# Attention as a software pipeline with an order fixed by hand on four engines, with scores as one float32 product and the sinks' values loaded later

## The chip, the cores and the metric

The kernel runs on one core of one Trainium2 chip. The metric is the device time of one execution in microseconds (us), 719.29 before the change. A core has TensorE (PE, the matrix engine), VectorE (DVE), ScalarE (ACT), GpSimd (POOL) and SyncE (SP, which here only issues DMA transfers). Each engine works through its own instructions in order; semaphores hold an instruction back until what it needs is there.

## The reference

Attention of 2 batches, 8 heads, 768 positions, 64 numbers a head; a query sees the last `window` keys (128) and the first `n_sink` (4). Then two MLPs over the 1,536 tokens. The weights come as float64.

```python
def _attn_ref(q, k, v, n_sink, window):
    scores = scale * np.matmul(q, k.transpose(0, 1, 3, 2))
    keep = (pos < n_sink) | ((rel >= 0) & (rel < window))
    scores = np.where(keep, scores, -1000000000.0)
    a = np.exp(scores - np.max(scores, axis=-1, keepdims=True))
    a = a / (np.sum(a, axis=-1, keepdims=True) + 1e-09)
    return np.matmul(a, v).astype(np.float32)
def _moe_ref(x, w_in, w_out):            # 512 -> 2048 -> 512
    h = x @ w_in
    return (h * (1.0 / (1.0 + np.exp(-1.702 * h))) @ w_out)
def _moe2_ref(x, w_gate, w_val, w_out):  # 512 -> 1536 -> 512
    return (1.0 / (1.0 + np.exp(-(x @ w_gate))) * (x @ w_val) @ w_out)
```

## The kernel before

**Attention** goes in 24 units: a batch b, a block t of 256 queries (3 to a batch) and a pair p of heads (4). A block of t > 0 has 272 columns of keys for each half of 128 queries (its window and 16 columns for the sinks); a first block (t = 0) has 128 and 256. A unit goes through four stages, each a generator:

- `st_a` (L241): four transposes bring q and k of the pair onto 64 partitions a head (tile tqk, L250). ScalarE casts them to the high part (L255), VectorE subtracts for the low part (L257); both stand in kq[p]. GpSimd copies the former block's last 128 keys (L246).
- `st_b` (L262): for each half e and head j the scores s are three products of parts, high with high, high with low, low with high (L278), the two heads in turn. VectorE adds the mask and takes the maximum (L283), ScalarE exponentiates and sums (L291), VectorE makes the reciprocal (L294, L295), GpSimd multiplies (L298) and copies the sinks' columns (L301).
- `st_c` (L305): four transposes of probabilities a head (three in a first block; tile tp, L315), copied to pt by ScalarE (L319), and one of the sinks' (ts, L324, psk, L327).
- `st_d` (L330): the values. o is a float32 product of v and pt for both heads, which fill different halves of o's partitions (L347); the last eight products of a unit are the sinks' with the tile vsk, on 32 rows each. ScalarE casts x to xh (L355), VectorE subtracts to xl (L357).

`load_vsink` (L167) sets vsk of a batch to zero and loads it. Every pass of the loop puts the four stages of four units in turn by the string `order`, with lags 0, 1, 3, 4; but the program is made with `TileContext(nc, schedule_with_timeline_sim=True)` (L725), and that scheduler puts each engine's instructions into an order of its own.

**Weights** come as blocks of four tiles of 128 x 512 (`weight_block`, L77): SP loads a raw tile of float64; ScalarE makes its absolute value (L100), VectorE builds float32 in three operations (L103 to L105), ScalarE casts to the high part (L107), GpSimd subtracts for the low part (L108). A product of the MLPs is `mm3` (L127), three matmuls of parts. The first block of w_in is converted in the attention loop (`W` in `order`).

**The MLPs.** `mlp_h(g)` (L359) multiplies the first block of w_in with 256 finished tokens: 48 matmuls of 256 columns (tile ha) and two copies to yacc (L372). Behind it come the other blocks of the first MLP: h (512 columns a matmul), silu, a split into two parts (L428, L429), and the second products y; then the second MLP in the same way. A block's second products are emitted behind the next block's first tile.

Of the kernel before, what the change touches and what calls it, by code (L numbers as in the profile page):

```python
# [8 lines left out]
F32 = mybir.dt.float32  # L9
# [29 lines left out]
def fast_path(ctx, tc, ident, nwv, any_, q, k, v, n_sink, window, w_in, w_out, w_gate, w_val, w_out2, out):  # L39
# [30 lines left out]
    # what the fast path rests on, checked at the end: the sizes of the weights'  # L70
    # exponents, and each row's maximum
# [5 lines left out]
    def weight_block(src, nm, pool):  # L77
        """A block's tiles, and the steps that fill them: float64 words to float32
        (exponent moved, mantissa cut to 24 bits), then hi + lo."""
        wh = pool.tile([P, 4, 512], F32R, tag="wh", name=f"wh_{nm}")  # L80
        wl = pool.tile([P, 4, 512], F32R, tag="wl", name=f"wl_{nm}")

        def load(i):
            raw = stg.tile([P, 512, 2], I32, tag="raw", bufs=2, name=f"raw_{nm}_{i}")
            nc.sync.dma_start(raw, src[:, i, :].bitcast(I32).rearrange("p (f t) -> p f t", t=2))
            return raw

        def steps():
            raws = [load(0)]
            yield  # L90
            for i in range(4):
                if i < 3:
                    raws.append(load(i + 1))
                raw = raws[i]
                lo, hi = raw[:, :, 0], raw[:, :, 1]
                w = stg.tile([P, 512], I32, tag="w", bufs=2, name=f"w_{nm}_{i}")
                wf = w.bitcast(F32)
                n = len(nbig)
                nbig.append(nm)
                nc.scalar.activation(wf, hi.bitcast(F32), AF.Abs, scale=2.0 ** -112,  # L100
                                     accum_out=big[:, n : n + 1])
# [39 lines left out]
    ps_t = es.enter_context(tc.tile_pool(name="ps_t", bufs=3, space=PSUM))  # L141
    ps_s = es.enter_context(tc.tile_pool(name="ps_s", bufs=3, space=PSUM))
# [4 lines left out]
    qk, vs, vsk = {}, {}, {}  # L147
# [18 lines left out]

    def load_vsink(b):  # L167
        """v of the sinks, for the rows (head of the pair, half of the block, sink)."""
        vsk[b] = ap_.tile([4 * NS, NPAIR, 2, D], F32, tag="vsk", bufs=1, name=f"vsk_{b}")
        nc.gpsimd.memset(vsk[b], 0.0)  # L170
        for j in range(2):
            for e in range(2):
                r = (2 * j + e) * NS
                nc.sync.dma_start(vsk[b][r : r + NS, :, e, :],
                                  v[b, j::2, :NS, :].rearrange("h s d -> s h d"))

# [62 lines left out]
    prs, pts, sks = {}, {}, {}  # L239

    def st_a(b, t, p):  # L241
        """q.T and k.T of a pair of heads, each in two parts."""
        qs, ks = qk[b, t]
        kk = kq[p]
        if t:
            nc.gpsimd.tensor_copy(kk[:, :, :P], f32(kk[:, :, C0 + P : C0 + QB]))  # L246
        tp = ps_t.tile([P, 2, QB], F32, tag="t", name=f"tqk_{b}_{t}_{p}")
# [5 lines left out]
        yield  # L253
        own = kk[:, :, C0:].rearrange("p s (u c) -> p s u c", u=2)
        nc.scalar.copy(own[:, 0], tp)  # L255
        yield
        nc.vector.tensor_tensor(own[:, 1], tp, f32(own[:, 0]), ALU.subtract)  # L257
        if t == 0:
            nc.gpsimd.tensor_copy(kk[:, :, P : P + NS], f32(kk[:, :, C0 : C0 + NS]))
        yield  # L260

    def st_b(b, t, p):  # L262
        """scores, and their softmax over the kept keys."""
        pr = prs[b, t, p] = ap_.tile([P, 2, 2, QB + NS], F32, tag="pr", bufs=2, name=f"pr_{b}_{t}_{p}")
        st = ap_.tile([P, 2, 2, 2], F32, tag="st", bufs=2, name=f"st_{b}_{t}_{p}")
        nm = nmax[:, (b * NQB + t) * NPAIR + p, :]
        if t:
            sks[b, t, p] = ap_.tile([P, 2, 2, NS], F32, tag="sk", bufs=3, name=f"sk_{b}_{t}_{p}")
        for e in range(2):
            mask = (me, mo)[e] if t else (m0, m1)[e]  # L270
            c0 = (e * P if t else C0)      # the first of the columns of keys
            n = QB + NS if t else (P if e == 0 else QB)
            ss = [ps_s.tile([P, QB + NS], F32, tag="s", name=f"s_{b}_{t}_{p}_{e}_{j}") for j in range(2)]
            qsl = slice(Q0 + e * P, Q0 + (e + 1) * P)
            for i, (qi, ki) in enumerate(((0, 0), (0, 1), (1, 0))):
                for j in range(2):
                    hd = slice(64 * j, 64 * j + 64)
                    nc.tensor.matmul(ss[j][:, :n], kq[p][hd, qi, qsl], kq[p][hd, ki, c0 : c0 + n],  # L278
                                     start=i == 0, stop=i == 2)
            yield  # L280
            for j in range(2):
                it = 2 * e + j
                nc.vector.tensor_tensor_reduce(  # L283
                    out=pr[:, j, e, :n], in0=ss[j][:, :n], in1=mask[:, :n], scale=-scale, scalar=3.4e38,
                    op0=ALU.add, op1=ALU.min, accum_out=nm[:, it : it + 1],
                )
            yield
            for j in range(2):
                it = 2 * e + j
                pt = pr[:, j, e, :n]  # L290
                nc.scalar.activation(pt, pt, AF.Exp, bias=nm[:, it : it + 1], scale=-1.0,  # L291
                                     accum_out=st[:, e, 0, j : j + 1])
                yield
            nc.vector.tensor_scalar(st[:, e, 1, :], st[:, e, 0, :], 1e-9, None, ALU.add)  # L294
            nc.vector.reciprocal(st[:, e, 1, :], st[:, e, 1, :])  # L295
            for j in range(2):
                pt = pr[:, j, e, :n]
                nc.gpsimd.tensor_scalar(pt, pt, st[:, e, 1, j : j + 1], 1.0, ALU.mult, ALU.mult)  # L298
            if t:
                at = P if e == 0 else 0  # L300
# [429 lines left out]
```

## Time and profile before

| | before |
|---|---|
| median of 3 runs | 719.29 us (719.19 to 719.37) |
| span of the profiled execution | 719.9 us |
| PE busy, matmuls | 704.8 us (98%), 3574 |
| VectorE busy | 392.9 us (55%) |
| ScalarE busy | 304.0 us (42%) |
| GpSimd busy | 161.3 us (22%) |

The profile is one execution; its own time is the span, from the first instruction to the last. The busy time of PE counts a matmul from its start to a modelled end, so that matmuls that follow each other overlap; starts are better marks than ends. The granted clock is a share of TensorE's full 2.4 GHz. A row of the view by lines tells the line, the engine, the operation, the tiles written and read, the shapes and the count, then busy time and mean ns; in a timeline a row has its start and its time in us.

### The profile page before, as it was taken

How to read it: one execution, taken by the hardware profiler on the slowest of the kernel's cores; microseconds unless marked ns; L12 is line 12 of the kernel's file. 1: busy time of each engine (PE TensorE's matmuls, PEld its weight loads, DVE VectorE, ACT ScalarE, POOL GpSimd, SP SyncE). 2: the span in 40 equal slices, each digit the busy share in tenths (PEclk: the TensorE clock that was granted, in tenths of full speed). 3: DMA queues.
4: the chain of work that ended last, by engine and by line, in shares of the span. 5: the costliest groups of instructions: out<-in, count | busy, mean ns of one | idle time of the engine just before them, and what ended most of it. 6: DMA issues, size and time to landing. Idle time of an engine off the chain costs nothing.

```text
span 719.9 us, 9655 instructions
## 1 busy us (share of the span) xinstructions
PE 704.8 (98%) x3574; PEld 562.1 (78%) x3574; DVE 392.9 (55%) x817; ACT 304.0 (42%) x714; POOL 161.3 (22%) x235
## 2 busy tenths in 40 slices
PE   7999999999999999999999999999998999999995
PEld 4667777778877788888888888888886888888884
DVE  5778766453999847835885781113774225222222
ACT  4787867666664424424443552223441203111110
POOL 4556653332232203101300220001330002000000
PEclk7899999999999999999999999999999999999998
DMA  9754572000333403400420140000441000001101
GB/s 213 157 132 108 149 168 81 2 1 1 102 119 106 141 1 100 135 1 1 145 89 0 60 144 32 1 0 1 147 146 60 0 1 1 0 20 40 39 21 63
DMA packets 49928, 49.08 MB, mean 68 GB/s; under 512 B 39504, under 2 KB 39760, under 8 KB 49872
## 3 DMA queue, kind: packets, MB, share of 16 engines
q1 hardware_dynamic: 49264, 48.24, 23.8%
q8 instruction: 30, 0.49, 0.3%
q14 instruction: 26, 0.21, 0.1%
q10 hardware_dynamic: 544, 0.13, 0.1%
q0 software_dynamic: 64, 0.00, 0.1%
HBM read 45.22 MB, written 3.15 MB: 67 GB/s over the span
## 4 chain that ended last, share of the span: by engine, by line
PE 80%; DVE 7%; DMA 7%; ACT 4%; issue 1%; POOL 1%; ACTq 0%; SPq 0%; POOLq 0%; DVEq 0%
PE s L278 6%; PE o L347 6%; PE g L129 4%; PE y L129 4%; PE y L130 4%; PE o L131 4%; PE o L129 4%; PE g L130 4%; PE o L130 4%; PE y L131 4%; PE g L131 4%; PE v L130 4%; PE v L129 4%; PE v L131 4%; PE tp L315 4%; PE h L129 3%
## 5 line engine op out<-in xcount | busy, mean ns | idle before, releaser
L480 DVE TENSOR_TENSOR sv<-v,sv 128x512 f32<-128x512 f32 x36 | 24.8, 689 | 113.8 <-PE v L131 113.8
L130 PE MATMUL y<-gl,wh_o 128*128 128x512 f32 x192 | 75.2, 393 | 0.3 <-DVE gl L429 0.3
L131 PE MATMUL y<-gh,wl_o 128*128 128x512 f32 x192 | 75.0, 391 | 0.0
L129 PE MATMUL y<-gh,wh_o 128*128 128x512 f32 x192 | 73.0, 394 | 0.9 <-DVE yacc L460 0.5
L479 ACT ACTIVATE sv<-g 128x512 f32<-128x512 f32 x36 | 21.4, 594 | 90.4 <-PE g L131 90.4
L298 POOL TENSOR_SCALAR pr<-pr,st 128x272 f32<-128x272 f32 (+2 forms) x96 | 47.8, 511 | 51.2 <-DVE st L295 23.1
L129 PE MATMUL o<-wh_p,gh_v 128*128 128x512 f32 (+1 forms) x148 | 57.1, 386 | 1.9 <-ACT gh_v L428 1.9
L130 PE MATMUL o<-wl_p,gh_v 128*128 128x512 f32 (+1 forms) x148 | 57.1, 386 | 0.0
L131 PE MATMUL o<-wh_p,gl_v 128*128 128x512 f32 (+1 forms) x148 | 57.1, 387 | 0.0
L129 PE MATMUL g<-xh,wh_g 128*128 128x512 f32 x144 | 57.0, 396 | 0.0
L130 PE MATMUL g<-xl,wh_g 128*128 128x512 f32 x144 | 56.8, 394 | 0.0
L131 PE MATMUL g<-xh,wl_g 128*128 128x512 f32 x144 | 56.7, 394 | 0.0
L131 PE MATMUL v<-xh,wl_v 128*128 128x512 f32 x144 | 56.5, 392 | 0.0
L130 PE MATMUL v<-xl,wh_v 128*128 128x512 f32 x144 | 56.5, 392 | 0.0
L129 PE MATMUL h<-xh,wh_i 128*128 128x512 f32 x144 | 56.5, 392 | 0.0
L129 PE MATMUL v<-xh,wh_v 128*128 128x512 f32 x144 | 56.5, 392 | 0.0
L131 PE MATMUL h<-xh,wl_i 128*128 128x512 f32 x144 | 56.4, 392 | 0.0
L130 PE MATMUL h<-xl,wh_i 128*128 128x512 f32 x144 | 56.4, 392 | 0.0
L428 ACT CAST gh_v<-sv 128x512 fp32r<-128x512 f32 x36 | 22.3, 620 | 78.8 <-DVE sv L480 75.7
L278 PE MATMUL s<-kq 64*128 64x272 f32 (+2 forms) x288 | 52.3, 335 | 1.8 <-DVE kq L257 1.1
L291 ACT ACTIVATE pr<-pr,nmax 128x272 f32<-128x272 f32 (+2 forms) x96 | 47.6, 498 | 14.6 <-DVE nmax L283 13.7
L108 POOL TENSOR_TENSOR wl_p<-w_p,wh_p 128x512 fp32r<-128x512 f32 x12 | 15.9, 1334 | 152.7 <-ACT wh_p L107 152.7
(138 smaller groups left out, 1531.6 us busy)
## 6 DMA issues: line engine op xcount, KB each, us to landing
raw_i<-in_moe_w_in_dram SPq DMA_DIRECT2D x16, 512.0 KB, 4.1
raw_o<-in_moe_w_out_dram SPq DMA_DIRECT2D x16, 512.0 KB, 3.2
raw_g<-in_moe_w_gate_dram SPq DMA_DIRECT2D x12, 512.0 KB, 3.6
raw_v<-in_moe_w_val_dram SPq DMA_DIRECT2D x12, 512.0 KB, 3.6
raw_p<-in_moe_w_out_dram SPq DMA_DIRECT2D x12, 512.0 KB, 3.3
v<-in_v_dram SPq DMA_DIRECT2D x12, 256.0 KB, 5.1
out_dram<-oacc SPq DMA_DIRECT2D x11, 256.0 KB, 2.0
k<-in_k_dram SPq DMA_DIRECT2D x10, 256.0 KB, 4.6
```

Source lines behind the costliest of these rows:

```text
L108: nc.gpsimd.tensor_tensor(wl[:, i, :], wf, f32(wh[:, i, :]), ALU.subtract)
L129: nc.tensor.matmul(ps, ah, bh, start=first, stop=False)
L130: nc.tensor.matmul(ps, ah, bl, start=False, stop=False)
L131: nc.tensor.matmul(ps, al, bh, start=False, stop=last)
L278: nc.tensor.matmul(ss[j][:, :n], kq[p][hd, qi, qsl], kq[p][hd, ki, c0 : c0 + n], start=i == 0, stop=i == 2)
L291: nc.scalar.activation(pt, pt, AF.Exp, bias=nm[:, it : it + 1], scale=-1.0, accum_out=st[:, e, 0, j : j + 1])
L298: nc.gpsimd.tensor_scalar(pt, pt, st[:, e, 1, j : j + 1], 1.0, ALU.mult, ALU.mult)
L315: nc.tensor.transpose(tp[:, o, :], pr[:, j, e, c0 : c0 + P], ident)
L347: nc.tensor.matmul(o[64 * j : 64 * j + 64, cs], vf(2 * p + j), pf(j), start=i == 0, stop=i == len(steps) - 1,)
L428: nc.scalar.copy(h, src)
L479: nc.scalar.activation(sg, pss[0], AF.Sigmoid)
L480: nc.vector.tensor_tensor(sg, pss[1], sg, ALU.mult)
```

## The change

A table of letters (ORDER) replaces the generators and their order string. A letter is one action on one engine with a lag in units: c, T, t copy the former keys, transpose q and k, copy tqk out; S, m, x the scores, maxima and exponentials of half 0 or 1; i, n the reciprocal and the multiplication; P, p transposes and copies of the probabilities of head 0 or 1; K, k the sinks'; V, h, l the values, xh and xl. An H1 (four in a step) gives a group of three ha matmuls, W a piece of a weight conversion. Inside `tc.manual_schedule` the instructions of PE, ACT, DVE and POOL keep the order in which they are written; SP's DMA issues, and all behind the loop, are the scheduler's as before.

```diff
+ORDER = "c-0 i-2 n-2 S0-1 S1-1 m0-1 m1-1 W1 x0-1 V-4 h-4 x1-1 T-0 t-0 H1 l-4 P0-3 H1 W1 p0-3 P1-3 p1-3 H1 H1 K-3 k-3 W1"
+LOADS = (2, 3)
+W_FROM = 4
...
-    ps_t = es.enter_context(tc.tile_pool(name="ps_t", bufs=3, space=PSUM))
-    ps_s = es.enter_context(tc.tile_pool(name="ps_s", bufs=3, space=PSUM))
+    ps_t = es.enter_context(tc.tile_pool(name="ps_t", bufs=2, space=PSUM))
+    ps_s = es.enter_context(tc.tile_pool(name="ps_s", bufs=4, space=PSUM))
...
-        vsk[b] = ap_.tile([4 * NS, NPAIR, 2, D], F32, tag="vsk", bufs=1, name=f"vsk_{b}")
-        nc.gpsimd.memset(vsk[b], 0.0)
+    vsk = kt_p.tile([P, NPAIR, 2, 2, D], F32, name="vsk")
+    sinks = [kt_p.tile([P, P], F32, name=f"sk{i}") for i in range(3)]
...
-    kq = [kt_p.tile([P, 2, Q0 + QB], F32R, name=f"kq{p}") for p in range(NPAIR)]
+    kq = [kt_p.tile([P, Q0 + QB], F32, name=f"kq{p}") for p in range(NPAIR)]
...
-        nc.scalar.copy(own[:, 0], tp)
-        nc.vector.tensor_tensor(own[:, 1], tp, f32(own[:, 0]), ALU.subtract)
+        nc.vector.tensor_copy(kk[:, C0:], tqs.pop(u).rearrange("p u c -> p (u c)"))
...
-            for i, (qi, ki) in enumerate(((0, 0), (0, 1), (1, 0))):
-                for j in range(2):
-                    nc.tensor.matmul(ss[j][:, :n], kq[p][hd, qi, qsl], kq[p][hd, ki, c0 : c0 + n],
-                                     start=i == 0, stop=i == 2)
+        for j in range(2):
+            nc.tensor.matmul(ss[j][:, :n], kq[p][hd, qsl], kq[p][hd, c0 : c0 + n], start=True, stop=True)
...
-            nc.vector.tensor_scalar(st[:, e, 1, :], st[:, e, 0, :], 1e-9, None, ALU.add)
-            nc.vector.reciprocal(st[:, e, 1, :], st[:, e, 1, :])
+        nc.vector.tensor_scalar(st[:, 1], st[:, 0], 1e-9, None, ALU.add)
+        nc.vector.reciprocal(st[:, 1], st[:, 1])
...
-            nc.scalar.copy(pt[:, o0:, :], tp[:, o0:, :])
+        (nc.vector.tensor_copy if j else nc.scalar.copy)(pt[:, o0:, :], tp[:, o0:, :])
...
-                              lambda h, e=e: vn[2 * NS * (h % 2) : 2 * NS * (h % 2 + 1), h // 2, e, :],
-                              lambda j: pt[2][2 * NS * j : 2 * NS * (j + 1), :]))
+                steps.append((slice(e * P, (e + 1) * P), lambda j, e=e: vsk[:, p, j, e, :], lambda j: ps))
...
+    with tc.manual_schedule(engines=engines):
+        for i in range(len(units) + last):
...
+            if u and u[1:] == (1, 0):
+                load_vsink(u[0])
+            for o in order:
+                if o[0] == "H":
+                    h_some(int(o[1:]), max(0, i - last) // NPAIR if w_done[0] >= W_ALL else 0)
+                elif o[0] == "W":
+                    if i >= W_FROM:
+                        w_some(int(o[1:]) * (2 if w_done[0] < W_ALL else 1))
```

Further: vsk and the sinks' tiles are set to zero once, with zero rows so that a sinks' product takes all 128 rows; vsk of a batch is loaded in step 4 and step 16, when the former batch's last unit (unit 11, in step 15) has read it, where before it was set and loaded with the batch's first block. pr has 3 buffers (2), pt 4 (3). Conversions of three blocks of weights (the first of w_in and of w_out, the second of w_in) run in the loop: two pieces for each W until the first block is through, then one, so that a tile takes two steps; VectorE's three operations on a tile are pieces of their own. The ha products stand in the loop from step 8 on, those of the last block behind it.

PE in the steady loop before, at the scores of batch 0's last block: tp are transposes of probabilities, s_2_1 and s_2_2 the scores of pairs 1 and 2 of the last block, kq keys and queries, ha the first MLP's products, tqk transposes of k and q.

```order
L278 MATMUL s_2_1_1_1_850<-kq_157 128x272 x3
L315 MATMUL tp_2_0_0_872<-ident,pr_2_0_724 128x128 x4
L278 MATMUL s_2_2_0_0_889<-kq_158 128x272
L278 MATMUL s_2_2_0_1_890<-kq_158 128x272
L131 MATMUL ha_1_2000<-xh_80,wl_i_161 128x256
L129 MATMUL ha_1_2000<-xh_80,wh_i_160 128x256
L130 MATMUL ha_1_2000<-xl_83,wh_i_160 128x256
L250 MATMUL tqk_2_3_880<-ident,k_2_491 128x128 x2
```

The same place after the change: a whole step's first half, where unit (2, pair 1) is scored.

```order
L291 MATMUL s_2_1_0_0_739<-kq_165 128x272
L291 MATMUL s_2_1_0_1_740<-kq_165 128x272
L291 MATMUL s_2_1_1_0_743<-kq_165 128x272
L291 MATMUL s_2_1_1_1_744<-kq_165 128x272
L384 MATMUL o_1_2_757<-pt_1_2_0_703,v_0_1_254 64x256
L384 MATMUL o_1_2_757<-pt_1_2_1_710,v_0_1_254 64x256
L384 MATMUL o_1_2_757<-pt_1_2_0_703,v_0_1_255 64x128
L384 MATMUL o_1_2_757<-pt_1_2_1_710,v_0_1_255 64x128
```

The first row of before shows three products of one head alone (x3): of 64 such triples of 272 columns, 51 stand as one row. After, four single products of two heads in turn stand together, and the values follow.

VectorE after the change in step 21: L305 are the maxima, L110, L112, L114 the three operations of a weight tile, L279 and L353 the copies out of tqk and tp.

```order
L305 ISA pr_2_1_1695,nmax<-s_2_1_1_0_1691,mo 128x272
L305 ISA nmax 128x1
L110 TENSOR_SCALAR w_o_0_2364<-w_o_0_2364 128x512
L305 ISA pr_2_1_1695,nmax<-s_2_1_1_1_1692,mo 128x272
L305 ISA nmax 128x1
L112 SCALAR_TENSOR_TENSOR w_o_0_2364<-raw_o_0_2360,w_o_0_2364 128x512
L114 SCALAR_TENSOR_TENSOR w_o_0_2364<-raw_o_0_2360,w_o_0_2364 128x512
L279 COPY kq_166<-tqk_2_2_1719 128x512
L398 TENSOR_TENSOR xl_85<-o_1_2_1705,xh_82 128x256
L110 TENSOR_SCALAR w_i_3_1701<-w_i_3_1701 128x512
L353 COPY pt_1_3_1_1746<-tp_1_3_1_1741 128x512
```

A tile of w_o that is written behind the loop (w_o_0_2364) has been put between a step's own operations; another stands so in step 23.

PE after the change behind the last unit's values: h is the first MLP's second block of features, ha_0_2037 and ha_1_2063 the last block of tokens, y the first second products.

```order
L384 MATMUL o_2_3_2005<-psk_2_3_2003,vsk 64x128 x4
L138 MATMUL ha_1_1973<-xh_82,wh_i_168 128x256
...
L138 MATMUL h_0_0_2396<-xh_80,wh_i_172 128x512
...
L140 MATMUL ha_0_2037<-xh_82,wl_i_169 128x256
L138 MATMUL h_0_2_2436<-xh_80,wh_i_172 128x512
...
L140 MATMUL ha_1_2063<-xh_82,wl_i_169 128x256
L138 MATMUL y_0_0_2134<-gh_0_0_2109,wh_o_170 128x512
```

Behind the values stand 12 matmuls of ha, then 48 of h and 48 of ha in turns of 27, 24, 21 and 24, and then y.

## Rows read from the trace of the kernel before

**Rows 1.** Busy time by stretches (us, count of each engine; then granted clock, DMA).

```profile
60.00:80.00 20.00, 20.00 (x174) 15.72 (x174) 15.05 (x47) 15.99 (x47) 13.21 (x23) 1.00 0.73 184
...
400.00:420.00 20.00, 20.00 (x88) 16.34 (x88) 16.42 (x25) 11.74 (x25) 7.29 (x6) 1.00 0.33 102
```

**Rows 2.** PE's waits over the whole span: us in total, times, longest.

```profile
PE o L129 <- ACT gh_v L428: 1.9, 1, 1.9
PE tqk L250 <- DMA k<-in_k_dram: 1.4, 2, 0.7
```

**Rows 3.** PE by line and form, 0 to 200 us: MLP matmuls of 512 columns.

```profile
L129 PE MATMUL y<-gh,wh_o 128*128 128x512 f32 x18 | 7.0, 389 | 0.0
...
L129 PE MATMUL h<-xh,wh_i 128*128 128x512 f32 x16 | 6.2, 390 | 0.0
```

**Rows 4.** PE's timeline, 60 to 63 us.

```profile
60.21 0.60 PE L315 MATMUL tp<-ident,pr 128*128 128x128 f32 x4
60.74 1.09 PE L347 MATMUL o<-pt,v 128*64 128x256 f32 x12
61.76 0.65 PE L347 MATMUL o<-psk,vsk 32*64 32x128 f32 x8
62.35 0.39 PE L129 MATMUL ha<-xh,wh_i 128*128 128x256 f32 x1
62.57 0.28 PE L130 MATMUL ha<-xl,wh_i 128*128 128x256 f32 x1
62.69 0.28 PE L131 MATMUL ha<-xh,wl_i 128*128 128x256 f32 x1
```

**Rows 5.** PE's timeline at scores, near 65 and 74 us.

```profile
64.67 0.64 PE L278 MATMUL s<-kq 64*128 64x272 f32 x3
65.24 0.66 PE L315 MATMUL tp<-ident,pr 128*128 128x128 f32 x4
...
73.61 0.65 PE L278 MATMUL s<-kq 64*128 64x272 f32 x6
74.18 0.43 PE L347 MATMUL o<-psk,vsk 32*64 32x128 f32 x2
```

**Rows 6.** VectorE's timeline, 61 to 63 us.

```profile
61.69 0.43 DVE L283 CUSTOM_DVE_ANT_0 pr<-s,mo 128x272 f32<-128x272 f32 x1
62.05 0.08 DVE L283 DVE_READ_ACCUMULATOR2_ANT nmax<- 128x1 f32 x1
62.05 0.69 DVE L257 TENSOR_TENSOR kq<-tqk,kq 128x512 fp32r<-128x512 f32 x1
62.65 0.77 DVE L105 SCALAR_TENSOR_TENSOR w_o<-raw_o,w_o 128x512 int32<-128x512 int32 x1
```

**Rows 7.** VectorE by line and form, 0 to 180 us: weight operations.

```profile
L105 DVE SCALAR_TENSOR_TENSOR w_i<-raw_i,w_i 128x512 int32<-128x512 int32 x8 | 7.6, 944 | 0.0
...
L104 DVE SCALAR_TENSOR_TENSOR w_i<-raw_i,w_i 128x512 int32<-128x512 int32 x8 | 6.1, 758 | 0.1
...
L105 DVE SCALAR_TENSOR_TENSOR w_o<-raw_o,w_o 128x512 int32<-128x512 int32 x6 | 4.7, 784 | 0.0
...
L103 DVE TENSOR_SCALAR w_i<-w_i 128x512 int32<-128x512 int32 x8 | 3.5, 435 | 1.4 <-ACT w_i L100 1.4
```

**Rows 8.** PE's timeline: the first value product and the first ts.

```profile
21.11 1.12 PE L347 MATMUL o<-pt,v 128*64 128x256 f32 x2
...
41.18 0.30 PE L324 MATMUL ts<-ident,sk 128*64 128x128 f32 x1
```

**Rows 9.** Timeline of GpSimd and VectorE near 66 us.

```profile
65.64 1.28 POOL L108 TENSOR_TENSOR wl_o<-w_o,wh_o 128x512 fp32r<-128x512 f32 x1 [0.35 <-ACT wh_o L107]
...
65.72 1.50 DVE L103 TENSOR_SCALAR w_o<-w_o 128x512 int32<-128x512 int32 x1
```

**Rows 10.** Busy time by stretches of 2 us, columns as in rows 1.

```profile
8.00:10.00 2.00, 0.88 (x8) 0.64 (x8) 1.81 (x11) 0.00 (x0) 1.07 (x5) 0.82 1.08 228
10.00:12.00 2.00, 2.00 (x10) 1.45 (x10) 0.94 (x6) 1.12 (x4) 0.26 (x1) 0.50 1.00 360
...
22.00:24.00 2.00, 2.00 (x15) 1.36 (x14) 1.76 (x5) 1.65 (x6) 0.76 (x2) 0.77 1.22 237
```

More of the change, by code (lines that the diff above doesn't have):

```diff
@@ L198, in fast_path @@
     load_v(*blocks[0])
-    mt = ap_.tile([P, 2, 2, QB + NS], F32, tag="pr", bufs=2, name="mt").rearrange("p a b c -> p (a b c)")
+    nc.gpsimd.memset(vsk, 0.0)
+    for sk in sinks:
+        nc.gpsimd.memset(sk, 0.0)
+    mt = ap_.tile([P, 2, 2, QB + NS], F32, tag="pr", bufs=3, name="mt").rearrange("p a b c -> p (a b c)")
     rel = mt[:, : QB + P]
@@ new lines, in s_max @@
+    def s_max(u, e):
+        b, t, p = u
+        if e == 0:
+            prs[u] = ap_.tile([P, 2, 2, QB + NS], F32, tag="pr", bufs=3, name=f"pr_{nid(u)}")
+            sts[u] = ap_.tile([P, 2, 2, 2], F32, tag="st", bufs=3, name=f"st_{nid(u)}")
+        n, _ = width(t, e)
+        mask = (me, mo)[e] if t else (m0, m1)[e]
+        ss = sss.pop((u, e))
+        nm = nmax[:, (b * NQB + t) * NPAIR + p, :]
+        for j in range(2):
+            it = 2 * e + j
+            nc.vector.tensor_tensor_reduce(
+                out=prs[u][:, j, e, :n], in0=ss[j][:, :n], in1=mask[:, :n], scale=-scale, scalar=3.4e38,
+                op0=ALU.add, op1=ALU.min, accum_out=nm[:, it : it + 1],
+            )
@@ new lines, in k_mm, with k_out, v_mm @@
+    def k_mm(u):
+        if u[1]:
+            tp = pss[u] = ps_t.tile([P, P], F32, tag="t", name=f"ts_{nid(u)}")
+            nc.tensor.transpose(tp, sinks[units.index(u) % 3], ident)
+    def k_out(u):
+        if u[1]:
+            ps = ap_.tile([P, P], F32, tag="psk", bufs=2, name=f"psk_{nid(u)}")
+            nc.scalar.copy(ps, pss[u])
+            pss[u] = ps
+    def v_mm(u):
+        b, t, p = u
+        pt, vc = pts.pop(u), vs[b, t]
+        prs.pop(u)
+        o = outs[u] = ps_o.tile([P, QB], F32, tag="o", name=f"o_{nid(u)}")
+        steps = [(slice(0, QB), lambda j: vc[0][:, 2 * p + j, :],
@@ L374, in fast_path, with v_place, v_hi, v_lo @@
-    wi, wi_steps = load_w(in_block(w_in, 0), "i0")
+                nc.tensor.matmul(o[64 * j : 64 * j + 64, cs], vf(j), pf(j),
+                                 start=i == 0, stop=i == len(steps) - 1)
+    def v_place(u):
+        b, t, p = u
+        tb, off = divmod((b * NQB + t) * QB, TB)
+        return p, tb, slice(off, off + QB)
+    def v_hi(u):
+        p, tb, dst = v_place(u)
+        nc.scalar.copy(xh[tb][:, p, dst], outs[u])
+    def v_lo(u):
+        p, tb, dst = v_place(u)
+        nc.vector.tensor_tensor(xl[tb][:, p, dst], outs.pop(u), f32(xh[tb][:, p, dst]), ALU.subtract)
@@ new lines, in mlp_h @@
+    def mlp_h():
+        for g in range(len(blocks)):
+            tb, off = divmod(g * QB, TB)
+            ts_ = slice(off, off + QB)
+            for f2 in range(GF // 2):
+                ps = ps_m.tile([P, 2, QB], F32, tag="m", name=f"ha_{g}_{f2}")
+                for i in range(2):
+                    f = 2 * f2 + i
+                    fs = slice(f * P, (f + 1) * P)
+                    for kk in range(KD):
+                        mm3(ps[:, i, :], wi[0][:, kk, fs], wi[1][:, kk, fs],
+                            xh[tb][:, kk, ts_], xl[tb][:, kk, ts_], kk == 0, kk == KD - 1)
+                        if i == 1 and kk == KD - 1:
+                            nc.scalar.copy(yacc[:, 2 * f2 : 2 * f2 + 2, g * QB : (g + 1) * QB], ps)
+                        yield g
@@ new lines, in fast_path @@
+    engines = {mybir.EngineType.PE, mybir.EngineType.Activation, mybir.EngineType.DVE, mybir.EngineType.Pool}
+    order = ORDER.split()
+    last = max(int(o.split("-")[1]) for o in order if "-" in o)
+    piece(w_steps, 1)
+    with tc.manual_schedule(engines=engines):
+        for i in range(len(units) + last):
+            if i == 2:
+                masks_after_first()
+            u = units[i] if i < len(units) else None
+            if u and u[2] in LOADS:
+                n = blocks.index(u[:2]) + 1
+                if n < len(blocks) and u[2] == LOADS[0]:
+                    load_qk(*blocks[n])
+                if n < len(blocks) and u[2] == LOADS[1]:
+                    load_v(*blocks[n])
+            if u and u[1:] == (1, 0):
[6 more added lines that the diff above has]
+                        w_some(int(o[1:]) * (2 if w_done[0] < W_ALL else 1))
+                else:
+                    what, lag = o.split("-")
+                    if 0 <= i - int(lag) < len(units):
+                        parts[what[0]](units[i - int(lag)], *map(int, what[1:]))
@@ L405, in fast_path @@
+    piece(w_steps, 99)
     es.close()
-    for g in range(len(blocks)):
-        mlp_h(g)
+    for _ in h_steps:
+        pass
     esg.close()
@@ L419, in load_w2 @@
     def load_w2(src, nm):
-        w, steps = load_w(src, nm)
-        for _ in steps:
+        w, loads = load_w(src, nm)
+        for _ in weight_steps(loads):
             pass
@@ L529, in drain @@
             f(*a)
-    wo = load_w2(out_block(w_out, 0), "o0")
+    wo = first[1][0]
     for g in range(1, NG1):
-        wi = load_w2(in_block(w_in, g), f"i{g}")
+        wi = first[2][0] if g == 1 else load_w2(in_block(w_in, g), f"i{g}")
         if g == 1:
```

246 lines of the change are left out of this document (101 added, 145 removed).

## The prediction

> **What bounds the kernel now.** I read the table by stretches first [rows 1]: TensorE (PE) is busy for 20.00 of 20 us from 60 to 80 us, where it runs attention, and from 400 to 420 us, where it runs the MLPs, at a granted clock of 1.00. The reader should not stop there, since ends of matmuls are modelled: what a matmul costs is the distance from its start to the next start. Second, what PE waited for [rows 2]: 1.9 us once in the second MLP and 1.4 us for k; the rest of the view are single waits of at most 1.2 us. So in both stages PE's own work sets the time, and a change pays if it takes PE time out. Third, where attention ends, though MLP work is already mixed in: before 200 us PE had run 100 matmuls of 512 columns (48 of h, 52 of y; [rows 3] has one of the three rows of each). 88 of them take 20 us [rows 1], 0.227 each, so the MLP had 22.7 us and attention with the first product (ha) had **177.3 us**. The 512-column matmuls behind that point stay as they are, so the forecast is a new value for these 177.3 us.
>
> **Prices on PE** are differences of starts. Transposes: 0.53 us for four (60.21 to 60.74) [rows 4], 0.11 each and 0.09 at the change to products that use half of the array's columns. ha: 0.12 each (62.57 to 62.69). The value product o is plain float32: 12 records of 1,024 paired columns in 1.02 us, where the two heads run beside each other, so about 0.86 ns a column and pair of heads, plus 0.15 to 0.2 for entering and leaving the mode; the sinks' 8 records, which switch the mode again, 0.59 us. Scores of today [rows 5]: three 272-column matmuls of one head take 0.57 us (64.67 to 65.24), six of two heads take the same 0.57 us (73.61 to 74.18). Of 64 such triples the scheduler left 51 to one head alone, as the first order listing shows.
>
> **The change, part by part.** A *step* is one pass of the new loop, 28 in all; in step i unit i is transposed, i-1 scored, i-3 has its probabilities transposed, i-4 is multiplied by v.
>
> *Scores.* One float32 matmul per head and half of the queries leaves two records, as o's do. For both halves and a pair of heads that is 4 x 272 columns at o's price: 0.94 + 0.16 = **1.10 us** per unit; 0.83 for first blocks, which have no previous keys (768 columns). No row shows float32 on halves of the array's rows beside each other; o shows it for halves of columns, and the six records above for halves of rows in another format. I take "beside each other"; if one after the other, 0.94 (0.66) more. [...]
> *Values.* vsk gets all 128 rows, so the mode switch inside o goes: 1,536 columns x 0.86 + 0.15 = **1.47** (from 1.61 in [rows 4]); 0.81 for first blocks.
> *Transposes.* q, k 0.49; probabilities 8 x 0.11 (6 in first blocks) = 0.88 or 0.66; sinks 0.20, else 0.09 for the switch. *ha*: four groups of three, 12 x 0.12 = 1.43, from step 8 on.
> So a full step costs PE 1.10 + 1.47 + 0.49 + 0.88 + 0.20 + 1.43 = **5.57 us**.
>
> *The other engines in such a step* [rows 6, 7]. VectorE: four maxima at 0.36 (distance of starts), the new copy of tqk and the second copy of pt, which moves here from ScalarE, 0.60 each (the 512-wide subtract's distance; 0.69 as a row), xl and the reciprocal pair some 0.4 each, the pair once instead of twice, half a weight tile (0.44 + 0.76 + 0.94)/2 = 1.07: **4.5 us**. ScalarE and GpSimd get nothing new. Today a unit takes (177.3 - 21.1)/24 = 6.5 us, with the first value product at 21.11 [rows 8]; 15.99 and 13.21 of 20 us [rows 1] are 5.2 and 4.3 in a unit. ScalarE loses two 512-wide operations, 0.6 each: 4.0. All are below 5.57, and the lags leave each result most of a step. Walking one step: scores 0 to 1.1, maxima done at 2.3, values to 2.6, T to 3.1, its copy to 3.9, second probabilities' copy about 5.5, needed by the next values at 6.7. No wait for PE; the nearest is the second copy, with 1.2 us to spare.
>
> *Steps 0 to 7* are not PE's. Before, the first value product starts at 21.11 us and the first ts at 41.18 [rows 8]. In the new order these are in steps 4 and 7. n_sink's masks and the first k arrive as before, and so the first score. I let step 4 begin at 19.3 us: four passes lose a subtract and two of three score products each, 0.45 us a pass. In steps 4 to 7 VectorE has a whole weight tile (2.1) and so 1.4 + 0.4 + 0.6 + 0.4 + 0.6 + 2.1 = 5.5, against 4.1 on PE. Four steps of 5.3 (the maxima of first blocks are shorter) give **40.5 us** for the start of step 8, about where ts stands now; 37 and 45 are the ends. The wider memset of vsk (twice the columns) stands on GpSimd among the first operations; PE waits for k there today, 0.7 us at the longest [rows 2], which covers it.
>
> *Steps 8 to 27* on PE: scores 13 x 1.10 + 4 x 0.83 = 17.6; q, k 16 x 0.49 = 7.8; probabilities 15 x 0.88 + 4 x 0.66 = 15.8; sinks 3.4; values 16 x 1.47 + 4 x 0.81 = 26.8; ha 20 x 1.43 = 28.6: **100 us**. Added: 1.8 us in steps 21 and 23, into which the scheduler puts a further weight tile of 2.1 on VectorE (the listing of VectorE: 4.5 + 2.1 is over 5.57); 2 us in steps 25 to 27, where PE has only 3 to 4 us and values wait for psk; the last block's ha behind the loop, 48 x 0.12 = 5.7.
>
> *Loads.* SP issues raw tiles as buffers come free; the first three blocks are converted at one tile per two steps (11 us), and two buffers are ahead of the conversion. vsk of the second batch is issued in step 16, when its last reader, unit 11 in step 15, is through; q and k queued behind it are needed in step 20. Cost nothing; if SP's order held them back, PE would stand in step 20.
> *After attention.* y's first products need four silu tiles, each a product and a split on VectorE; the last listing puts 48 matmuls of h and 48 of ha ahead of them, 0.227 and 0.12 each, 17 us. Cost nothing.
>
> **Sum.** 40.5 + 100 + 1.8 + 2 + 5.7 = 150.0 against 177.3: 27.3 us less. The profiled execution's span is 719.9, 0.6 above the median of the runs; from the median, 719.29 - 27.3 = **692.0 us**.
>
> **Rivals.**
> *B, scores of the two heads one after the other*: + 13 x 0.94 + 4 x 0.66 = 14.9, 707 us. For: no row has it. Against: the six records, and o's pairs.
> *C, VectorE held up by GpSimd.* A shift of w took 1.50 us while GpSimd ran its 1.28 us subtract, against 0.44 on average of w_i's eight [rows 9, 7]. With every weight operation at such a price (1.5 + 1.2 + 1.2), steps 4 to 7 take 7.3 (+8), full steps 5.4 to 5.7, still PE's; with the thin steps +12: 704 us. GpSimd is busy for up to 4.3 of 5.57 us in the new step, now for 13.21 of 20 [rows 1]; a little more, so the averages should nearly hold. The Trainium skill (SBUF — State Buffer, "Who interferes with whom") calls the port that the two share an exclusive lock for a whole instruction; by that rule this rival's prices are the normal case whenever both run, and the 1.50 row agrees, the average of 0.44 does not.
> *D, slower than now: the clock.* The granted clock was 0.82 from 8 to 10 us, where PE was busy for 0.88 of 2 us, 0.50 (1.2 GHz) from 10 to 12, and rose only in the stretch from 22 to 24 [rows 10]. Work at 1.2 GHz takes twice as long. In steps 1 to 7 PE has 17 us of work in 36, so the clock may stay low, or fall again. It decides at 27.3 us of PE work, that is 55 us of attention at the low level beyond the start; if it lasted through step 19 (about 59 us of work), 751 us. Against: in the later stretches of [rows 1] it was 1.00 with the same kinds of matmul, and from step 8 PE is never without work.
> *E, the gain is given back in the first MLP*, since conversions and silu crowd VectorE there: up to 5 us, 697. Against: by 180 us the present kernel had finished 14 tiles (8 of w_i, 6 of w_o, [rows 7]), and the new loop has 14 as well, so what is left for VectorE is the same.
> That the order is not kept is excluded by the listings.
>
> **Numbers.** A, as summed, 0.70; B 0.09, C 0.11, D 0.05, E 0.05. Range: start 37 to 45, added terms 0 to 6, so A is 686 to 700; two us below for the price of o and scores, and up to 705 for E and C: 684 to 705, which leaves out B, D and a little of A. Of no change (0.2%, 1.4 us, what a measurement here can tell) 0.01; slower 0.05 from D; faster 0.94.
>
> **What would show it.** Right: PE's distance from one T to the next near 5.6 us in steps 8 to 13 and 20 to 23; the four score records of a half in 0.5 us; first K near 40, last value product near 145 us. B: 1.0 us for a half. C: VectorE's weight rows above 1 us and maxima that follow them late. D: clock 0.50 beyond 45 us. Wrong altogether: PE waiting for pt or psk in full steps, which the walk through the step excludes.

## The result and the profile after

The changed kernel takes **695.01 us** (median of 4 runs, 693.93 to 695.55; before 719.33), a ratio of 0.963 with a 95% interval of 0.958 to 0.968. The profiled execution has a span of 693.8 us against 719.9.

TensorE (PE) by stretches, columns as in [rows 1] (behind the length: PE, its weight loads, VectorE, ScalarE, GpSimd; then the granted clock):

```profile
60.00:80.00 20.00, 20.00 (x201) 16.64 (x200) 15.91 (x57) 14.05 (x48) 11.58 (x25) 1.00 0.49 114
157.00:162.00 5.00, 0.34 (x4) 0.14 (x2) 5.00 (x8) 3.63 (x7) 1.33 (x1) 0.99 0.32 107
162.00:166.00 4.00, 4.00 (x11) 3.22 (x12) 4.00 (x6) 2.20 (x5) 1.49 (x1) 0.59 0.45 135
166.00:170.00 4.00, 4.00 (x19) 3.29 (x18) 3.31 (x7) 1.27 (x3) 1.80 (x1) 1.00 0.42 131
```

From 60 to 80 us PE gets through 201 matmuls where it had 174 [rows 1]; their kinds differ, so the length of a step, below, says more. New is a hole behind attention: from 157 to 162 us PE works for 0.34 of 5 us, and in the 4 us after it the granted clock is 0.59, which lets through 11 matmuls of 512 columns where 17.6 fit at 0.227 us each: 1.5 us lost.

PE's waits, as in [rows 2]:

```profile
PE s L291 <- DVE kq L279: 4.7, 3, 2.6
PE y L138 <- ACT yacc L415: 4.7, 1, 4.7
PE tp L347 <- DVE kq L279: 4.3, 5, 1.0
PE o L138 <- ACT gh_v L500: 2.2, 1, 2.2
```

All waits for kq lie before 40 us, but for one near 116 us. One full step in the timeline (start, time):

```profile
49.57 1.19 PE L291 MATMUL s<-kq 64*128 64x272 f32 x8
50.69 1.09 PE L384 MATMUL o<-pt,v 128*64 128x256 f32 x12
51.61 0.61 PE L384 MATMUL o<-psk,vsk 128*64 128x128 f32 x8
52.15 0.44 PE L266 MATMUL tqk<-ident,k 128*128 128x128 f32 x2
52.91 0.69 DVE L279 COPY kq<-tqk 128x512 f32<-128x512 f32 x1 [1.04 <-POOL sk L336]
52.99 0.60 PE L347 MATMUL tp<-ident,pr 128*128 128x128 f32 x4
53.79 0.60 PE L347 MATMUL tp<-ident,pr 128*128 128x128 f32 x4
54.93 0.28 PE L360 MATMUL ts<-ident,sk 128*128 128x128 f32 x1
55.14 1.19 PE L291 MATMUL s<-kq 64*128 64x272 f32 x8
```

From scores to scores are 55.14 - 49.57 = 5.57 us, and PE waits nowhere in it. A bank is here one buffer of a pool that the kernel places in PSUM; tqk, the two tp and ts of a step share the two of ps_t. The second tp, which needs the bank that tqk leaves, starts at 53.79, when VectorE's one copy (52.91, 0.69 us) has just ended.

### The profile page after: what moved, and what is told of

Its sections match the earlier page's. It is cut to its first block, busy times and chain, and to the rows that moved or that the text cites. A ratio compares the mean times of both kernels' runs of the same rounds, so it can differ in the third digit from the quotient of the medians.

```text
span 693.8 us, 9345 instructions
## 1 busy us (share of the span) xinstructions
PE 669.1 (96%) x3478; PEld 543.2 (78%) x3478; DVE 393.6 (57%) x793; ACT 279.4 (40%) x666; POOL 163.2 (24%) x237
## 4 chain that ended last, share of the span: by engine, by line
PE 84%; DVE 7%; DMA 3%; ACT 2%; issue 1%; POOL 1%; SPq 0%; ACTq 0%; POOLq 0%; DVEq 0%
PE y L138 6%; PE y L139 6%; PE y L140 6%; PE o L140 4%; PE o L138 4%; PE h L138 4%; PE h L139 4%; PE h L140 4%; PE o L139 4%; PE g L138 4%; PE g L139 4%; PE g L140 4%; PE v L140 4%; PE v L139 4%; PE v L138 4%; PE o L384 4%
## 5 line engine op out<-in xcount | busy, mean ns | idle before, releaser
L332 POOL TENSOR_SCALAR pr<-pr,st 128x272 f32<-128x272 f32 (+2 forms) x96 | 50.1, 536 | 25.5 <-DVE st L323 16.4
L317 ACT ACTIVATE pr<-pr,nmax 128x272 f32<-128x272 f32 (+2 forms) x96 | 47.2, 494 | 19.3 <-DVE nmax L305 18.9
L138 PEld LDWEIGHTS y<-gh,wh_o 128*128 128x128 f32 x192 | 36.5, 190 | 12.8 <-ACT yacc L415 4.9
```

The source lines that it names most:

```text
L332: nc.gpsimd.tensor_scalar(pt, pt, st[:, 1, e, j : j + 1], 1.0, ALU.mult, ALU.mult)
```

## Experiments

In the diffs - is the changed kernel (or the one named), + the run; they show the lines that matter. Each ratio is to runs of the kernel before on the same chip; across chips only ratios are compared.

**The changed kernel again.** 

> The changed kernel again, as it is, beside the next two on the same chip: 0.960 to 0.968 of the kernel before, so that differences of half a per cent between variants can be told.

Measured: 696.24 us, 0.9652 (0.9632 to 0.9672). This and 0.9631 are what the variants are held against.

**Three products of parts, in the new order.** Into the changed kernel go the former cast, subtract and scores:

```diff
-        nc.vector.tensor_copy(kk[:, C0:], tqs.pop(u).rearrange("p u c -> p (u c)"))
+        nc.scalar.copy(own[:, 0], tp)
+        nc.vector.tensor_tensor(own[:, 1], tp, f32(own[:, 0]), ALU.subtract)
...
+        for i, (qi, ki) in enumerate(((0, 0), (0, 1), (1, 0))):
```

> The changed kernel with the scores as before (three products of high and low parts, the cast on ScalarE, the subtract on VectorE), but in the new fixed order, the two heads in turn (pt has 2 buffers for room, its copies stand behind the values anyway). Theory (the order pairs the heads, and that is what makes scores cheap): six products of two heads took 0.57 us in the profile of before, two halves 1.14, against 1.12 for the float32 scores of the changed kernel, so a full step stays within 0.2 us of 5.57 and the time is 695 to 700 us. Rival (the gain comes from one product in place of three): scores cost three times as much as float32, or as much as one head alone before (0.57 us for each head and half, 2.28 a unit), the step grows by 1.1 us and the time is 712 to 720 us.

Measured: 720.36 us, 1.0016 (1.0005 to 1.0026): the whole gain is gone. But not for the rival's reason. PE's waits and the timeline of a step there:

```profile
PE tp L352 <- ACT pt L358: 13.1, 12, 2.2
PE tp L352 <- DVE kq L282: 10.1, 9, 1.7
```

```profile
62.19 1.01 PE L295 MATMUL s<-kq 64*128 64x272 f32 x12
63.13 1.09 PE L389 MATMUL o<-pt,v 128*64 128x256 f32 x12
...
64.59 0.44 PE L266 MATMUL tqk<-ident,k 128*128 128x128 f32 x2
...
65.49 0.51 ACT L322 ACTIVATE pr<-pr,nmax 128x272 f32<-128x272 f32 x1
...
66.00 0.57 ACT L281 CAST kq<-tqk 128x512 fp32r<-128x512 f32 x1
...
66.46 0.59 ACT L358 COPY pt<-tp 128x512 f32<-128x512 f32 x1
66.60 0.69 DVE L282 TENSOR_TENSOR kq<-tqk,kq 128x512 fp32r<-128x512 f32 x1 [2.20 <-ACT kq L281]
...
67.11 0.65 PE L352 MATMUL tp<-ident,pr 128*128 128x128 f32 x4 [0.71 <-ACT pt L358]
```

Twelve products take 0.94 us (62.19 to 63.13), *less* than the four float32 ones (1.12). What costs is the late cast: on ScalarE it stands behind the second half's exponentials (66.00, though tqk was there at about 65.3), and behind it come ScalarE's copy of the first tp (66.46) and VectorE's subtract (66.60). The second tp waits for one of these two, whichever holds its bank: in this step for the copy (it starts at 67.11, before the subtract has ended), in other steps for the subtract. The two waits are 23.2 us in all. A full step takes mostly 6.3 to 6.6 us. Both theories fall; a third, the late cast, was tested by the next run, and the ring of two banks by the two after it.

**The cast ahead of the exponentials.**

```diff
-ORDER = "... x0-1 V-4 h-4 x1-1 T-0 t-0 H1 l-4 ..."
+ORDER = "... x0-1 V-4 h-4 T-0 t-0 x1-1 H1 l-4 ..."
```

> The run with three score products in the new order (720 us, its ring of two banks as there), with one thing moved: ScalarE casts tqk before the second half's exponentials, no longer behind them. Theory (that run lost its time because the cast stood behind the exponentials in ScalarE's order, and VectorE's subtract and all that follows it in VectorE's order stood behind the cast): the second probabilities wait for nothing, a full step takes 5.35 to 5.6 us (scores took 0.94 us there against 1.12), 690 to 698 us, so the format of the scores is worth nothing by itself. Rival (two operations in turn to empty tqk are too long in any order): steps stay above 6.0 us, 708 to 720 us.

Measured: 708.55 us, 0.982 (0.980 to 0.984): half of the loss is back, most full steps take 5.9 to 6.1 us. The rest shows in PE's waits, which at tp are now all for the subtract, and in the timeline, where cast and subtract follow at once and still take 1.3 us in turn:

```profile
PE tp L352 <- DVE kq L282: 11.6, 21, 1.6
```

```profile
67.19 0.59 ACT L281 CAST kq<-tqk 128x512 fp32r<-128x512 f32 x1 [0.26 <-PE tqk L266]
...
67.81 0.69 DVE L282 TENSOR_TENSOR kq<-tqk,kq 128x512 fp32r<-128x512 f32 x1 [0.88 <-ACT kq L281]
...
68.55 0.65 PE L352 MATMUL tp<-ident,pr 128*128 128x128 f32 x4 [0.31 <-DVE kq L282]
```

Of the 12.3 us between this run and the changed kernel on the same chip, 6.7 lie before step 8 (45.7 against 39.0 us); 5.7 us of the wait for the subtract lie there too.

**Another bank for the second tp.**

```diff
-        tp = tps[u, j] = ps_t.tile([P, 4, P], F32, tag="t", name=f"tp_{nid(u)}_{j}")
+        pool, tag = (ps_s, "s") if j else (ps_t, "t")
+        tp = tps[u, j] = pool.tile([P, 4, P], F32, tag=tag, name=f"tp_{nid(u)}_{j}")
```

With three products: 

> As the run with three score products in the new order (720 us), but the second head's transposed probabilities take their PSUM bank from the pool of the scores, no longer from the two banks that tqk, both heads' probabilities and the sinks share. Theory (that run lost its time in the ring of two banks: tqk is free only after ScalarE's cast and VectorE's subtract in turn, and the second probabilities wait for its bank): the wait of 1.0 to 1.5 us in a step goes, a full step takes 5.3 to 5.6 us (scores took 0.94 us there against 1.12), the time is 692 to 700 us. Rival (ScalarE is too full with the cast, whatever the bank): steps stay above 6.2 us and the time above 712.

Measured: 715.22 us, 0.990 (0.989 to 0.992). Neither forecast fits: the time is in the rival's range, the steps are shorter than it had them. The wait for tqk's bank went, and the scores wait instead for the second tp's copy, which stands behind the late subtract on VectorE (full steps 5.7 and 6.1 us in turn):

```profile
PE s L295 <- DVE pt L359: 8.7, 14, 1.5
```

In the changed kernel: 

> The changed kernel with the same move of the second probabilities to the pool of the scores. Theory (its full steps have no wait for the ring, since one copy by VectorE frees tqk early; only steps 4 to 7 have 4.3 us of such waits, beside a busy VectorE): 692 to 695 us, full steps at 5.57 as before. Rival (a fifth tile in a pool of four lets the scores wait): 697 to 705 us.

Measured: 697.19 us, 0.965 (0.963 to 0.966), full steps at 5.57 us: nothing is gained there.

**Without the fixed order.**

```diff
-    with tc.manual_schedule(engines=engines):
+    if True:
```

> The changed kernel without the fixed order: the same instructions, ordered by the scheduler. Theory (the order carries the gain): the scheduler again parts the two heads of scores and lets ha products stand where they fall; the time goes back by over half of the gain, 708 to 719 us. Rival (the products carry it: float32 scores, no mode switch inside the values, fewer casts): 693 to 700 us.

Measured: 706.26 us, 0.980 (0.978 to 0.983). This lies between the two forecasts. Against 0.963 to 0.965 the fixed order is worth 11 to 12 us, somewhat under half of the gain; the rest stays even in the scheduler's order, which starts from the new table. What that order does to values, in PE's timeline:

```profile
88.46 0.39 PE L138 MATMUL ha<-xh,wh_i 128*128 128x256 f32 x1
88.89 0.65 PE L384 MATMUL o<-pt,v 128*64 128x256 f32 x2
89.46 0.39 PE L139 MATMUL ha<-xl,wh_i 128*128 128x256 f32 x1
```

One head's value product takes 0.57 us between ha products (88.89 to 89.46); six products of both heads, two of 256 columns and four of 128, took 1.02 [rows 4]. The scores it hardly parted, against the theory: at least 104 of their 128 records of 272 columns stand in rows of eight, the two heads together. How the 11 to 12 us divide was not tried.

**Float32 scores alone**, in the kernel before:

```diff
-            for i, (qi, ki) in enumerate(((0, 0), (0, 1), (1, 0))):
...
+            for j in range(2):
+                nc.tensor.matmul(ss[j][:, :n], kq[p][hd, qsl], kq[p][hd, c0 : c0 + n], start=True, stop=True)
```

> The kernel before with nothing changed but its scores: one float32 product a head and half, copied once by VectorE. Theory (the order carries the gain): the scheduler leaves most products to one head alone, so a float32 product costs its own full time, about 0.45 us against 0.57 for three of the other format; 96 pairs of halves gain at most some 10 us, 709 to 717 us. Rival (the products carry it): 20 us or more, 695 to 700 us.

Measured: 732.02 us, 1.021 (1.017 to 1.026), slower than either theory had it. PE's timeline:

```profile
79.90 0.72 PE L275 MATMUL s<-kq 64*128 64x272 f32 x2
80.55 0.44 PE L311 MATMUL tp<-ident,pr 128*128 128x128 f32 x2
```

One float32 product of one head takes 0.65 us (79.90 to 80.55), more than the three of the other format (0.57, [rows 5]), and most of them stand alone here (44 of 57 rows of 272 columns hold one product). Alone it is a loss; beside the other head, in the changed kernel, a product costs 0.28 (1.12 for four).

**The sinks on 64 rows**, 32 to a product:

```diff
-    vsk = kt_p.tile([P, NPAIR, 2, 2, D], F32, name="vsk")
+    vsk = kt_p.tile([4 * NS, NPAIR, 2, 2, D], F32, name="vsk")
```

> The changed kernel with the sinks' values and probabilities on 64 rows, 32 to a product, as before the change. Theory (a product on fewer rows switches TensorE's mode inside the values: eight sinks' records took 0.59 us in the profile of before): a step with sinks grows by 0.14 us, 16 such steps by 2.2 us, 696.5 to 698 us. Rival (the number of rows costs nothing): 694.5 to 695.6 us.

Measured: 698.12 us, 0.966 (0.964 to 0.968), which the intervals don't part from the changed kernel. The rows do: values from 45.69 to 47.29 us are 1.60, against 1.46 (50.69 to 52.15) above; in 16 steps that is 2.2 us. From one T to the next a full step takes 5.73 us in place of 5.57.

```profile
45.69 1.09 PE L385 MATMUL o<-pt,v 128*64 128x256 f32 x12
46.70 0.65 PE L385 MATMUL o<-psk,vsk 32*64 32x128 f32 x8
47.29 0.44 PE L266 MATMUL tqk<-ident,k 128*128 128x128 f32 x2
```

**The hole at 157 us.** The timeline of the changed kernel there:

```profile
158.41 2.35 DVE L520 TENSOR_TENSOR sg<-yacc,sg 128x512 f32<-128x512 f32 x2
158.88 1.33 POOL L119 TENSOR_TENSOR wl_i<-w_i,wh_i 128x512 fp32r<-128x512 f32 x1 [3.54 <-ACT wh_i L117]
...
160.79 0.62 ACT L500 CAST gh<-sg 128x512 fp32r<-128x512 f32 x1 [1.05 <-DVE sg L520]
...
161.32 0.58 ACT L415 COPY yacc<-ha 128x512 f32<-128x512 f32 x1
...
161.95 0.80 PE L138 MATMUL y<-gh,wh_o 128*128 128x512 f32 x1 [4.66 <-ACT yacc L415]
```

The first y waits for the copy of the last ha tile, that copy stands behind two casts of silu on ScalarE, and the casts wait for VectorE. VectorE's pair of products at 158.41 takes 2.35 us beside GpSimd's subtract; at 141.37, ahead of GpSimd's next subtract, such a pair took 1.29. ScalarE stood 1.05 us for that before its second cast (160.79), so about 1 us of the wait of 4.7 goes back to GpSimd.

```diff
+    ps_y.tile([P, TB], F32, tag="y", name="y_skip")
```

> The changed kernel with one unused tile taken from the pool of the y products, so that the first y tile does not take the bank of PSUM that the last ha tile holds until ScalarE has copied it to yacc; nothing else is moved on TensorE. Theory (the stall of 4.9 us at 157 us is a wait for that bank, and the lower clock that follows it comes from the stall): both go, 4.9 us and about 2 us of matmuls at the lower clock, 687 to 690 us. Rival (VectorE, busy for 18.7 of 20 us there, is the bound of that stretch): the stall comes back at the next silu tile or y copy, 693 to 696 us.

Measured: 695.6 us, 0.967 (0.966 to 0.969): nothing moved, the same wait of 4.7 us. The unused tile did not help; that y waits for the bank is not shown by this run.

```diff
-    esg.close()
+    ctx.callback(esg.close)
...
-    ps_y = ctx.enter_context(tc.tile_pool(name="ps_y", bufs=4, space=PSUM))
+    ps_y = ctx.enter_context(tc.tile_pool(name="ps_y", bufs=3, space=PSUM))
```

> The changed kernel with the pool of the ha tiles kept open, so that its bank goes to no other pool (three y tiles in place of four). Theory (the y products' stall of 4.9 us at 157 us is a wait for that bank, which any y tile of a pool laid over it inherits, and the lower clock follows from the stall): both go, 687 to 690 us. Rival (VectorE is the bound of that stretch: it is busy for 18.7 of 20 us): the stall comes back at the next y products or silu tiles, 692 to 696 us.

Measured: 694.38 us, 0.961 (0.959 to 0.963). Now y starts before the last ha (151.78 and 159.54 us), so the bank was what held it; and the time comes back later, with VectorE full up to 190 us and a lower clock at 200 (stretches, columns as above):

```profile
160.00:180.00 20.00, 19.44 (x86) 15.69 (x85) 20.00 (x31) 12.42 (x24) 6.41 (x4) 1.00 0.31 105
180.00:190.00 10.00, 9.52 (x42) 7.40 (x41) 9.96 (x16) 4.02 (x10) 2.58 (x2) 1.00 0.29 107
190.00:200.00 10.00, 8.88 (x39) 6.96 (x38) 8.60 (x13) 4.23 (x11) 4.37 (x3) 1.00 0.49 155
200.00:204.00 4.00, 3.42 (x11) 2.54 (x12) 3.97 (x6) 3.41 (x7) 1.69 (x2) 0.77 0.43 136
```

To compare such losses I take the time from the last value product's start to 260 us, less 0.227 us for each 512-column matmul started by 260 us and 0.119 for each ha behind that product: 3.7 us before, 8.0 in the changed kernel, 6.9 here.

**Less for VectorE, and a busy start.** First the y copies to ScalarE:

```diff
-                nc.vector.tensor_copy(ya, ps)
+                nc.scalar.copy(ya, ps)
```

> The changed kernel with the pool of the ha tiles kept open (as in the run before with that) and the twelve first y tiles copied to yacc by ScalarE in place of VectorE, 0.68 us each. Theory (from 160 to 210 us VectorE is the bound: it was busy for 20.00 of 20 us there, and taking the stall at 157 us away only moved it to 184 to 201 us): 8 us less on VectorE, the waits and the lower clock at 200 us mostly go, 3 to 6 us less than with the pool alone, 0.951 to 0.956 of the kernel before. Rival (ScalarE then holds up silu, or the order of the copies and not VectorE's load is what matters): 0.958 to 0.965.

Measured: 694.77 us, 0.964 (0.962 to 0.966); the loss stays at 7.1 us, as the rival had it. Then, on top:

```diff
+                    if what == "T" and i < 3:
+                        for _ in range((8, 3, 2)[i]):
+                            nc.tensor.matmul(wps, wz[:, :P], wz, start=True, stop=True)
...
+            if nm.split("_")[0] not in ("o1", "i2", "o2", "i3"):
                 nc.vector.scalar_tensor_tensor(w, lo, 29, w, ALU.logical_shift_right, ALU.bitwise_or)
```

> The run with the ha tiles' pool kept open and the first y tiles copied by ScalarE, with two further edits that act in stretches apart. First, 8, 3 and 2 matmuls of zeros (bfloat16, 512 columns, as the 8 at the start) behind the transposes of steps 0, 1 and 2, where TensorE waits 2.9, 1.7 and 1.2 us. Theory (the clock falls at 8 us because TensorE stands idle there): it stays at 1.00 through the first 20 us, scores of steps 1 to 3 take 1.1 us in place of 1.58, and step 8 begins 1 to 3 us earlier than in that run's profile (39.5). Rival (the clock falls all the same): 0.50 from 10 to 18 us and step 8 begins as late or later. Second, the last of VectorE's three operations on a weight tile (0.68 us) is left out for the 16 tiles of four blocks (second and third of w_out, third and fourth of w_in), so that their weights lack the low 3 bits of 24. Theory (VectorE's load is the bound behind attention): 11 us less of it, and of the waits and low clock from 165 to 205 us (7.1 us lost up to 260 us, beside the matmuls themselves) at most 4 us stay. Rival (what binds is the chain from silu through ScalarE's cast to VectorE's subtract, not the load): 6 to 7 us stay. Both theories right: 0.955 to 0.959 of the kernel before; both rivals: 0.963 to 0.966.

Measured: 690.91 us, 0.956 (0.954 to 0.958). The loss behind attention falls from 7.1 to 4.8 us: VectorE's load is a part of it, not all; what makes up the other 4.8 us was not taken apart. As to the start, the stretches of the changed kernel and then of this run:

```profile
6.00:8.00 2.00, 0.03 (x2) 0.03 (x2) 1.62 (x9) 0.00 (x0) 0.02 (x1) 1.00 1.10 234
8.00:10.00 2.00, 2.00 (x12) 1.35 (x12) 1.69 (x6) 0.00 (x0) 1.07 (x4) 0.57 1.20 246
...
16.00:18.00 2.00, 2.00 (x10) 1.35 (x9) 1.38 (x9) 1.59 (x7) 1.17 (x3) 0.50 1.31 223
```

```profile
6.00:8.00 2.00, 0.90 (x5) 0.19 (x2) 1.55 (x9) 0.00 (x0) 0.00 (x0) 1.00 1.11 239
8.00:10.00 2.00, 1.97 (x15) 1.20 (x15) 1.68 (x6) 0.00 (x0) 1.02 (x4) 1.00 1.17 225
10.00:12.00 2.00, 0.47 (x5) 0.28 (x6) 2.00 (x13) 1.80 (x8) 0.43 (x2) 1.00 0.88 259
```

The clock stays at 1.00 up to 30 us, and step 4 begins at 17.3 us (19.6 in the run with y on ScalarE). Yet step 8 begins at 39.5 in both. Just before step 6 SP issues raw weights, at 24.77, and ScalarE starts on the tile at 29.98:

```profile
24.77 2.89 SPq L90 DMA_DIRECT2D raw_i<-in_moe_w_in_dram  x2
...
29.98 0.66 ACT L107 ACTIVATE w_i<-raw_i 128x512 f32<-128x512 f32 x1 [2.07 <-POOL pr L333]
```

VectorE's first weight operation waits for that tile, its copy of tqk stands behind, and step 6 takes 7.0 us in place of 5.0. The row names GpSimd, but the trace has the transfer land 5.1 us after its issue, at 29.9, when ScalarE had been free for 2 us: the landing held it. PE then stands from 30 to 32 us, and the clock falls after all:

```profile
30.00:40.00 10.00, 7.83 (x36) 5.10 (x38) 7.69 (x21) 7.91 (x26) 5.95 (x13) 0.66 0.44 128
```

In the run with y on ScalarE it is 1.00 from 30 to 40 us. Step 7 takes 6.5 us in place of 5.7, so the late weights and the lower clock behind them take back what the start gained. Neither was tried alone.

No variant that computes everything is clear of the changed kernel: 0.961 and 0.964 with the bank kept, against 0.963 and 0.965.

## Why the prediction was right, and where it was off

Forecast 692.0, measured 695.01, within 684 to 705. The main path, A, came true; of the rivals E took part, and C a little. That the total is only 3 us off is in part luck, since the errors below have both signs.

- *Steps on PE*: right to the hundredth, 5.57 forecast, 5.56 to 5.57 in eight steps, but by terms that cancel. Measured (forecast): scores 1.12 (1.10), values 1.46 (1.47), sinks 0.21 (0.20). Two terms were too dear, q, k 0.41 (0.49) and probabilities 0.71 (0.88). One was too cheap, ha 1.67 (1.43), since a group of three that follows another format costs 0.44 and not 0.36. "Beside each other" holds and rival B is out: a half of the scores takes 0.56 us. The Trainium skill (TensorEngine Tiling (Array Packing), "Key Properties") says that different tiles of the array can execute matmuls in parallel, and names no format there; for float32 the trace agrees, with these 0.56 us.
- *Steps 0 to 7*: step 4 began at 19.1 (19.3 forecast), step 8 at 38.4 (40.5). VectorE worked for 18.8 of the 19.3 us between, 4.7 a step where the forecast had 5.3.
- *The added 1.8 us*: 1.07, once, in the step of the VectorE listing (6.64 us; counted from 0 it is step 22, not 21). The last value product began at 138.7 ("near 145"). Attention's part, with all its ha, ends at 157.1 less 0.227 for each of the 48 h before it, that is 146.2; the forecast was 150.0.
- *"After attention ... Cost nothing"* is the step that failed, and the gain was given back in the first MLP, as rival E had it. The 17 us of cover were there, but they cover silu, not the bank that the last ha tile holds nor the ScalarE queue in front of its copy. The 467 matmuls of 512 columns that PE had started by 260 us leave 153.9 us for all else, so 153.9 - 146.2 = 7.7 us are given back, and with the bank freed most of it was lost all the same, with VectorE full (6.9 of 8.0 by the other count). The kernel before has 180.7 by the same count at 260 us; it loses 180.7 - 177.3 = 3.4 around its own y products from 200 us on, which the forecast left out. So 27.3 + 3.8 + 3.4 - 7.7 = 26.8 at 260 us, and 26.1 at the end.
- *The offset of the profile* was mis-set: 719.9 is a span, and in the profile after the span, 693.8, is 1.75 below its own execution's time, 695.55. If the same holds before, that profiled execution stood 2.3 above its median, not 0.6; 26.1 in the profiles are 24.3 in the medians.
- *Rival C*: in steps 4 to 7 the three weight operations took 0.44, 0.69 and 0.75 us on average, not 1.5, 1.2 and 1.2. GpSimd paid too: its copy of 128x32, 0.21 us undisturbed, took 0.71 beside a VectorE operation (32.41 and 32.44 below). The Trainium skill (SBUF — State Buffer, "Who interferes with whom") says that whoever issues first holds the port and the other waits; these rows agree, and so does the 2.35 us pair at 158.41 beside GpSimd's subtract. But "whenever both run" was too wide: that pair reads yacc, and where the same product reads h, out of PSUM, it took 0.69 us beside GpSimd's subtracts (at 242.21).

```profile
32.41 0.68 DVE L112 SCALAR_TENSOR_TENSOR w_i<-raw_i,w_i 128x512 int32<-128x512 int32 x1
32.44 0.71 POOL L336 COPY sk<-pr 128x32 f32<-128x32 f32 x1
```

- *Rival D*: the clock was at its low level to 18 us and 1.00 from 20, so it decided nothing. The run with a busy start shows why little was at stake: weights that land late come next, and behind them the clock falls again.
- *What the prediction had no eye for*: it read "plain float32 scores" as a saving on PE. On PE they are a small loss against paired products of parts (1.12 to 0.94). They pay because tqk is emptied by one operation on VectorE in place of two in turn; in a fixed order with two banks a late cast goes round the whole step, as the run with three products and the one with the cast moved show.

## What to carry to other kernels

In a fixed order, price a change not only by its engine time but by how long it keeps a PSUM bank and who stands behind it in each queue: a second operation in the chain that empties a bank cost 12 to 26 us here, by where it stood in its queue, though the products that came with it were cheaper on TensorE. Matmuls that use half of the array belong side by side; look in the trace whether the scheduler left them so. Where a phase ends early, look at which bank and which queue the next phase's first tile inherits, and at the engine that becomes full there.

## What the runs showed of the hardware

- A float32 score product of one head took 0.65 us alone and 0.28 beside the other head's; three products of the other format took 0.57 alone, and six of a pair 0.47 in the new order (0.94 for twelve).
- In the changed kernel PE stood from 5.3 to 8.0 us; the granted clock was 0.57 from 8 to 10 us and then 0.50 (1.2 GHz) to 18 us. With 8, 3 and 2 matmuls of zeros (512 columns) in the gaps of the first three steps it stayed at 1.00 up to 30 us, with PE busy for 0.47 of 2 us from 10 to 12; behind the 2 us from 30 to 32 in which PE did nothing it fell again (0.66 on average from 30 to 40). Behind the hole at 157 us it was 0.59 over 4 us.
- VectorE's 128x512 product of silu took 1.75 us beside GpSimd's subtract where it read yacc and sg, both in SBUF (159.01, the second of the pair at 158.41), and 0.69 beside it where one input was h, in PSUM (242.21).
